# Output rounds two steps earlier, with the row halves turned over at every gap: a fused convolution and ELU layer on one core

## The chip, the cores and the metric

One core of one Trainium2 chip runs the kernel. The metric is the device time of one execution in microseconds (us); for a kernel it is the median over its runs. A core has five engines that work side by side and meet only at semaphores: PE (matrix products; its weight loads, PEld, overlap the products), ACT, DVE, POOL, and SP, which here only issues DMAs. DMAs run on 16 shared DMA engines. PE writes its results to PSUM, from where ACT and DVE read them.

## What is computed

Input `x` is 8 x 4096 tokens of 192 channels. A causal convolution of 7 taps runs along the tokens, with one softmaxed set of taps for each of 8 heads of 24 channels. Its result (32768 tokens x 192) goes through a layer of width 2048 with ELU and back to 192:

```python
w = softmax(weight, axis=-1)                     # 8 heads x 7 taps
out = np.einsum('hk,bskhg->bshg', w, x_unf)      # x_unf: 7 shifted views of x, zero-padded in front
h = x @ w_in                                     # x: the line above, 32768 x 192; w_in: 192 x 2048
g = np.where(h > 0.0, h, np.exp(np.minimum(h, 0.0)) - 1.0)
return g @ w_out                                 # w_out: 2048 x 192
```

## The kernel before

**Tiling.** The tokens are cut into 32 super-tiles `s` (later also `t`) of 1024 tokens, each of two groups `g` of 512. The width 2048 is cut into 16 chunks `q` of 128. A *step* `n` = 16 s + q makes the first product for one super-tile and one chunk, so there are 512 steps. PE's 128 rows are used as two halves of 64 rows that work at the same time (`tile_position`).

**One step.** PE makes a *pair* (L647): six matrix products of 512 columns, three for each token group, out of `att` and `w_in` into one of three slots of `H` in PSUM. ACT takes exp of both groups (L438, two instructions into `E`), POOL clamps them (L355), DVE forms the ELU in `gT` from `E` and from the same slot of `H` (L501). A slot may be written again when DVE has read it (`wait_slot`, semaphore `s_tt`).

**Output rounds.** The second product sums over the 16 chunks. Its unit is the *round* (L677): for a super-tile `t`, a half of its tokens (`half`, 256 tokens of each group), a chunk `q` and a block `kb` of 128 tokens, two matrix products of 192 columns side by side. Row half `rt` multiplies its 64 rows of the chunk's `gT` with its 64 rows of `w_out` and adds into PSUM bank `g` of `ops`. In the first *orientation* row half 0 works for group 0 and row half 1 for group 1; in the second they are exchanged, so that each group gets all 128 rows of the chunk. A bank may not be written by both row halves at once, so a change of orientation (a *turn*) waits until the last round before it has been written (`s_swap`). One half of a super-tile needs 16 chunks x 2 blocks x 2 orientations = 64 rounds, and ACT then copies `ops` to `osb` (L409) and SP issues two output DMAs (L267). `ops` is single: the next half's first round waits for that copy (`s_oev`).

**Order.** The list `order`, written out before the program, sets the order of work on all engines; each engine follows it in turn. Rounds of super-tile `t` go into the gaps between pairs from step 16 (t + 1) + LAG on, with LAG = -1: `HALF_STEPS` gives (10, 10, 6, 6, 10, 11, 11) rounds to seven gaps, the eighth has none, and then the second half follows the same way. All 32 rounds of the first orientation come first (10 + 10 + 6 + 6), so the turn falls between the fourth and the fifth gap, behind a pair.

**Convolution.** A conv (L620) is 40 small matrix products for one group of one super-tile, out of `xg` (tokens, loaded by POOL's DMAs, L307) and `Tr` (taps). ACT copies the result to `csb` (L418), SP writes it to `conv_slots` in DRAM (L711) and, once that has landed, reads it back rearranged into `att` by three DMAs (L279). `m` = 2 s + g - 2 counts the convs; super-tile 0 is made in another way at the start. `CONV_AT` places two convs in each super-tile, at its steps 4 and 12; each splits the eleven-round gap that it falls in (5 rounds, conv, 6 rounds). `EARLY_CONV` places the first three: after the pairs of steps 5, 9 and 16. The first `FREE_CONV` = 2 of them use the two banks of `ops`, which no round needs yet, and ACT copies each in two halves, the second behind the next step's exp; later convs take a slot of `H`. `X_AT` places POOL's loads of `xg`.

**Start.** In the first steps, where there are no rounds, PE gets pairs of idle products (`warm_pair`, L538) that only keep it busy. They write into `ops` and so wait for the copy of an early conv.

**SP's queue** at the start is, in order: the taps, a copy of a part of `w_in` (L704), the write of conv 0 (L711), the three reads of it (L279), the write of conv 1, the three reads of that. Each waits in turn; the pair of step 16 needs all six reads.

**End.** The last half (t = 31, half 1) accumulates in a slot of `H`; ACT copies group 0 (L401), DVE group 1 (L512), and SP and ACT issue one output DMA each.

Of the kernel before, what the change touches and what calls it, by code (L numbers as in the profile page):

```python
# [12 lines left out]
P = 128  # L13
# [13 lines left out]
NXB = 2  # L27
NE = 4
NG3 = 2
LAG = -1  # L30
WCOLS = ((0, 256), (256, 640), (640, 1280), (1280, 2048))
Q_PART = (0,) * 2 + (1,) * 3 + (2,) * 5 + (3,) * 6
WARM = (9, 1)
HALF_STEPS = (10, 10, 6, 6, 10, 11, 11)

CONV_AT = ((4, 1, 1), (12, 2, 0))
EARLY_CONV = {5: (1, 0), 9: (1, 1), 16: (2, 0)}
FREE_CONV = 2
QUAD = 4
XTW = 136  # L40
HALO = 2
XW = 5
X_AT = ((5, 1), (10, 0), (13, 2))

PIECES = (
    ((0, 0, CW, 0), (1, 0, CW, CW), (2, 0, CW, 2 * CW), (3, 0, CW, 3 * CW), (4, 0, 24, 4 * CW)),
# [5 lines left out]
def bass_lightweight_conv__then__act_elu_kernel(  # L52
# [13 lines left out]
    NT = Bsz * S  # L66
    assert S % SUP == 0 and tuple(out.shape) == (NT, D)
    NQ = FF // FC
    NR = 4 * NQ
    assert NQ == 16  # L70
    NS = NT // SUP
    SPB = S // SUP
# [3 lines left out]
    x_flat = x.rearrange("b s d -> (b s) d")  # L76


    steps = []
    slot_of_pair, slot_of_conv, prior = {}, {}, []  # L80
    occupant = [None, None, None]

# [4 lines left out]
        return k  # L87

    order = []
    last_half = (NS - 1, 1)  # L90
    last_slot = None

    def conv_at(s, g):
        m = 2 * s + g - 2
# [1 line left out]
            slot_of_conv[m] = take_slot(("c", m))  # L96
        order.append(("c", m))

    rounds_at = {}
    for t in range(NS):  # L100
        base = NQ * (t + 1) + LAG
        for half in range(2):
            r = 0
            for i, cnt in enumerate(HALF_STEPS):
                rounds_at[base + 8 * half + i] = (t, half, r, r + cnt)
                r += cnt
            assert r == NR
    for n in range(NP + NQ + LAG):
        s, i = divmod(n, NQ)
        if n < NP:  # L110
            slot_of_pair[n] = take_slot(("h", n))
            order.append(("h", n))
        convs = [EARLY_CONV[n]] if n in EARLY_CONV else []
        if s:
            convs += [(s + ahead, g) for at, ahead, g in CONV_AT if at == i and n < NP]
        convs = [(k, g) for k, g in convs if k < NS]
        if n in rounds_at:
            t, half, r0, r1 = rounds_at[n]
            if (t, half) == last_half and r0 == 0:
                last_slot = take_slot(None)  # L120
            mid = (r0 + r1) // 2 if convs else r1
            order.append(("o", t, half, r0, mid))
            for k, g in convs:
                conv_at(k, g)
            if mid < r1:
                order.append(("o", t, half, mid, r1))
        else:
            for k, g in convs:
                conv_at(k, g)


    taps = nc.dram_tensor("conv_taps", (HEADS, ZW), BF16).ap()
    bounce = nc.dram_tensor("conv_slots", (2, 2, P, SUP), BF16).ap()

    with ExitStack() as stack:
# [68 lines left out]
        s_dw = [sema(f"s_dw{i}") for i in range(4)]  # L204
        s_band = sema("s_band")
        s_att = [sema(f"s_att{i}") for i in range(2)]
        s_mm2 = sema("s_mm2")
        s_swap = sema("s_swap")
        s_oev = sema("s_oev")
        s_out = [sema(f"s_out{i}") for i in range(2)]  # L210
# [43 lines left out]
        def conv_read(W, m):  # L254
            W(s_ce, m + 1)

        def out_group(eng, t, half, g):
            b = (2 * t + half) % 2
            row = SUP * t + GS * g + 2 * P * half
            dst = out[row : row + 2 * P, :].rearrange("(k p) d -> p k d", p=P)  # L260
            if t == 0:
                dst = bass.AP(
                    tensor=out.tensor,
                    offset=(GS * half + 1 - g) * D,
                    ap=[[QUAD * D, P], [2 * D, 2], [1, D]],
                )
            eng.dma_start(dst, osb[:, b, g, :, :]).then_inc(s_out[b], 16)  # L267
# [97 lines left out]
        def _scalar(a):  # L365
# [26 lines left out]
            a.activation(  # L392
                att[:, 0, 2, 0 : GS // 2], H[:, 0, 0 : GS // 2], ACT.Copy
            ).then_inc(s_ha)
            def evac(t, half):
                n_half = 2 * t + half
                W(s_mm2, n_half + 1)
                b = n_half % 2
                W(s_out[b], 32 * (n_half // 2))
                if (t, half) == last_half:  # L400
                    a.activation(  # L401
                        osb[:, b, 0, :, :].rearrange("p k d -> p (k d)"),
                        H[:, last_slot % 3, 0 : 2 * D],
                        ACT.Copy,
                    ).then_inc(s_oev)
                    W(s_od, 1)
                    out_group(a, t, half, 1)
                    return
                a.activation(  # L409
                    osb[:, b, :, :, :].rearrange("p g k d -> p g (k d)"),  # L410
                    ops[:, :, 0 : 2 * D],
                    ACT.Copy,
                ).then_inc(s_oev)
# [8 lines left out]
            for item in order:  # L422
                if item[0] == "c":
                    m = item[1]
                    W(s_cv, m + 1)
                    W(s_dw[m % 4], 16 * (m // 4))
                    if m < FREE_CONV:
                        conv_evac(m, 0, 1)
                        late.append(m)
                    else:  # L430
                        conv_evac(m, 0, 2).then_inc(s_ce)
                elif item[0] == "h":
                    n = item[1]
                    k = slot_of_pair[n] % 3
                    W(s_h, n + 1)
                    W(s_tt, 2 * (n - NE) + 2)
                    for u in range(2):
                        a.activation(  # L438
                            E[:, n % NE, u, :], H[:, k, GS * u : GS * (u + 1)], ACT.Exp
                        ).then_inc(s_exp)  # L440
                    if late:
                        conv_evac(late.pop(), 1, 2).then_inc(s_ce)
                else:
                    _, t, half, r0, r1 = item
                    if r1 == NR:
                        evac(t, half)

        @block.vector
        def _vector(v):
# [45 lines left out]
            for n in range(NP):  # L495
                s, q = divmod(n, NQ)
                if s >= NG3:
                    W(s_mm2, 2 * (s - NG3 + 1))
                for u in range(2):
                    W(s_clp, 2 * n + u + 1)  # L500
                    v.scalar_tensor_tensor(  # L501
# [5 lines left out]
                        op1=ALU.max,  # L507
                    ).then_inc(s_tt)
            b = (2 * NS - 1) % 2
            W(s_mm2, 2 * NS)  # L510
            W(s_out[b], 32 * (NS - 1))
            v.tensor_copy(  # L512
                osb[:, b, 1, :, :].rearrange("p k d -> p (k d)"),
                H[:, last_slot % 3, GS : GS + 2 * D],
            ).then_inc(s_od)

        @block.tensor
        def _tensor(pe):
# [61 lines left out]
            for j in range(3):  # L580
# [18 lines left out]
                            tile_position=(HP * r, 0),  # L599
                        )  # L600
                ins.then_inc(s_hc)
            for item in order:
                if item[0] == "c":
                    m = item[1]
                    s, g = divmod(m + 2, 2)
# [23 lines left out]
                elif item[0] == "h":  # L629
                    n = item[1]  # L630
                    s, q = divmod(n, NQ)
                    if n == 0:
                        W(s_ha, 2)
                        W(s_hd, 2)
                    elif n < NQ - 1 and not any(n - 2 <= e < n for e in EARLY_CONV):
                        conv_read(W, sum(e < n for e in EARLY_CONV) - 1)
                        warm_pair(WARM[1])
                    if Q_PART[q] < 3:
# [15 lines left out]
                            )  # L654
                    ins.then_inc(s_h)
                else:
                    _, t, half, r0, r1 = item
                    W(s_w[4], 16)
                    if (t, half) == last_half:
                        acc = H[:, last_slot % 3, :].rearrange("p (g t) -> p g t", g=2)  # L660
                        if r0 == 0:
                            wait_slot(last_slot)
                    else:
                        acc = ops
                        if r0 == 0:
                            conv_read(W, FREE_CONV - 1)
                            W(s_oev, 2 * t + half)
                    for r in range(r0, r1):

                        second, (q, kb) = r // (NR // 2), divmod(r % (NR // 2), 2)  # L670
                        W(s_tt, 2 * (NQ * t + q) + 2)
                        if second:
                            W(s_swap, 2 * (2 * t + half + 1))
                        t0 = 2 * P * half + P * kb
                        for rt in range(2):
                            g = rt ^ second
                            ins = pe.matmul(  # L677
                                acc[:, g, D * kb : D * (kb + 1)],
                                gT[HP * rt : HP * (rt + 1), t % NG3, q, g, t0 : t0 + P],
                                w_out[HP * rt : HP * (rt + 1), q, :],  # L680
                                start=(r == 0),
                                stop=(r == NR - 1),
                                tile_position=(HP * rt, 0),
                            )
                            if r == NR // 2 - 1:
                                ins.then_inc(s_swap)
                    if r1 == NR:
                        ins.then_inc(s_mm2)

        @block.sync  # L690
        def _sync(sy):
# [14 lines left out]
            for item in order:  # L706
# [14 lines left out]
                        W(s_h, NQ * s)  # L721
                        read_att(sy, W, s + 1, 0)
                elif item[0] == "o":
                    _, t, half, r0, r1 = item
                    if r1 < NR:
                        continue
                    W(s_oev, 2 * t + half + 1)
                    for g in range(1 if (t, half) == last_half else 2):
                        out_group(sy, t, half, g)
            for b in range(2):  # L730
                sy.wait_ge(s_out[b], 32 * NS)


# [26 lines left out]
```

## Time and profile before

| | before |
|---|---|
| median of 7 runs | 753.16 us (751.25 to 754.46) |
| the profiled execution: its own time, its span | 753.79 us, 752.0 us |
| busy PE / ACT / DVE / POOL over the span | 737.0 / 646.9 / 635.3 / 662.0 us |
| rounds into `ops`, L677 | 8064 products, 415.3 us |
| pairs, L647 | 3072 products, 407.4 us |
| convs into `H`, L620 | 2400 products, 39.7 us |
| ELU on DVE, L501 | 1024 x 680 ns |
| exp on ACT, L438 | 1024 x 605 ns |

The span runs from the first to the last instruction; the execution's own time has 1.8 us more around it. The end of a product is modelled and products overlap in the pipeline, so what a stretch of PE work costs is read from the start of one group to the start of the next, not from its busy time. PEld is the weight load, which PE pulls ahead of the products where nothing holds it.

### The profile page before, as it was taken

What the parts mean: (1) busy time and instruction counts of PE and PEld (TensorE: products, weight loads), DVE (VectorE), ACT (ScalarE), POOL (GpSimd) and SP (SyncE); (2) the same over time, 40 slices, a digit from 0 to 9 for tenths busy, and PEclk for the clock granted to TensorE, in tenths of its full rate; (3) what the DMA queues carried; (4) which work ended last, traced back from release to release, by engine and by line L of the source; (5) the groups of instructions that cost most, each with busy time, mean ns of one, the idle gap of its engine ahead of it and who ended that gap; (6) DMA issues with size and microseconds to landing.
All of it is one profiled execution on the core that took longest, in us unless ns stands there. A gap on an engine that the chain in (4) does not pass through costs nothing.

```text
span 752.0 us, 32224 instructions
## 1 busy us (share of the span) xinstructions
PE 737.0 (98%) x13858; PEld 512.0 (68%) x13858; DVE 635.3 (84%) x1041; ACT 646.9 (86%) x1163; POOL 662.0 (88%) x1107
## 2 busy tenths in 40 slices
PE   8699999999999999999999999999999999999997
PEld 4376766766766766766667667667667767767676
DVE  5778898898898888898888898888898888888893
ACT  6788888888888888888888888888888888889882
POOL 8779899899899899899898998998998998998882
PEclk9999999999999999999999999999999999999999
DMA  9535345445345345345344345354355344355112
GB/s 176 105 85 117 80 96 118 81 96 116 76 100 117 79 100 108 83 101 117 77 102 103 87 102 114 79 104 95 92 105 111 76 108 91 91 110 107 59 44 65
DMA packets 107006, 72.79 MB, mean 97 GB/s; under 512 B 44520, under 2 KB 106608, under 8 KB 106864
## 3 DMA queue, kind: packets, MB, share of 16 engines
q1 hardware_dynamic: 66224, 54.37, 23.8%
q0 software_dynamic: 40224, 15.78, 19.5%
q8 instruction: 108, 1.77, 1.0%
q10 hardware_dynamic: 416, 0.59, 0.2%
q14 instruction: 34, 0.28, 0.1%
HBM read 44.78 MB, written 41.42 MB: 115 GB/s over the span
## 4 chain that ended last, share of the span: by engine, by line
PE 95%; DMA 2%; DVE 1%; ACT 1%; SPq 0%; issue 0%; POOL 0%
PE ops L677 45%; PE H L647 44%; PE H L620 5%; DVE gT L501 1%; DMA conv_slots<-csb 1%; PE H L677 1%; DMA att<-conv_slots 0%; DMA xf<-in_x_dram 0%; SPq L279 0%; ACT E L438 0%; PE H L589 0%; POOL E L355 0%; PE ops L589 0%; DVE xh L476 0%; ACT csb L418 0%
## 5 line engine op out<-in xcount | busy, mean ns | idle before, releaser
L501 DVE SCALAR_TENSOR_TENSOR gT<-E,H 128x512 f16<-128x512 f32 x1024 | 629.9, 680 | 99.0 <-POOL E L355 91.1
L355 POOL TENSOR_SCALAR E<-E 128x512 f32<-128x512 f32 x1024 | 605.5, 615 | 74.8 <-ACT E L438 72.5
L438 ACT ACTIVATE E<-H 128x512 f32<-128x512 f32 x1024 | 545.9, 605 | 86.0 <-PE H L647 72.5
L677 PEld LDWEIGHTS ops<-w_out,gT 64*128 64x128 f16 x8064 | 342.7, 94 | 109.9 <-ACT osb L409 10.8
L677 PE MATMUL ops<-w_out,gT 64*128 64x192 f16 x8064 | 415.3, 243 | 0.9 <-DVE gT L501 0.9
L647 PE MATMUL H<-att,w_in 64*128 64x512 bf16 x3072 | 407.4, 378 | 6.6 <-DMA att<-conv_slots 2.8
L647 PEld LDWEIGHTS H<-att,w_in 64*128 64x128 bf16 x3072 | 130.2, 94 | 107.0 <-DVE gT L501 4.9
L418 ACT ACTIVATE csb<-H 128x1024 bf16<-128x1024 f32 x60 | 61.4, 1024 | 0.7 <-PE H L620 0.7
L409 ACT ACTIVATE osb<-ops 128x768 f32<-128x768 f32 x63 | 51.5, 817 | 5.1 <-PE ops L677 5.1
L307 POOL DMA_DIRECT2D xg<-in_x_dram x62 | 52.2, 842 | 0.4 <-issue 0.4
L620 PE MATMUL H<-Tr,xg 128*24 128x122 bf16 (+1 forms) x2400 | 39.7, 210 | 0.0
L620 PEld LDWEIGHTS H<-Tr,xg 128*24 128x24 bf16 x2400 | 30.4, 92 | 9.6 <-issue 9.6
L512 DVE COPY osb<-H 128x384 f32<-128x384 f32 x1 | 0.6, 559 | 8.9 <-PE H L677 8.9
L677 PE MATMUL H<-w_out,gT 64*128 64x192 f16 x128 | 5.6, 243 | 0.1
L538 PE MATMUL ops<-zw 64*128 64x512 bf16 x20 | 3.9, 378 | 1.9 <-ACT csb L418 1.9
L677 PEld LDWEIGHTS H<-w_out,gT 64*128 64x128 f16 x128 | 5.2, 94 | 0.3 <-PE H L677 0.3
L533 PE MATMUL ops<-zw 128*128 128x512 bf16 x9 | 4.0, 625 | 1.2 <-DVE zw L451 1.2
L312 POOL DMA_DIRECT2D w_in<-in_moe_w_in_dram x7 | 4.6, 658 | 0.3 <-DMA wh<-in_weight_dram 0.3
L401 ACT ACTIVATE osb<-H 128x384 f32<-128x384 f32 x1 | 0.5, 491 | 4.7 <-PE H L677 4.7
L538 PEld LDWEIGHTS ops<-zw 64*128 64x128 bf16 x20 | 1.0, 94 | 3.7 <-ACT csb L418 2.8
L533 PEld LDWEIGHTS ops<-zw 128*128 128x128 bf16 x9 | 1.2, 142 | 3.2 <-issue 1.9
L418 ACT ACTIVATE csb<-ops 128x512 bf16<-128x512 f32 x4 | 2.5, 619 | 0.0
(46 smaller groups left out, 25.6 us busy)
## 6 DMA issues: line engine op xcount, KB each, us to landing
out_dram<-osb SPq DMA_DIRECT2D x127, 192.0 KB, 2.7
conv_slots<-csb SPq DMA_DIRECT2D x62, 256.0 KB, 2.5
att<-conv_slots SPq DMA_DIRECT2D x186, 64.0 KB
xg<-in_x_dram POOLq DMA_DIRECT2D x31, 240.0 KB, 5.1
xg<-in_x_dram POOLq DMA_DIRECT2D x31, 192.0 KB, 4.5
w_out<-in_moe_w_out_dram POOLq DMA_DIRECT2D x1, 768.0 KB, 14.5
w_in<-in_moe_w_in_dram POOLq DMA_DIRECT2D x2, 240.0 KB, 8.0
xf<-in_x_dram ACTq DMA_DIRECT2D x1, 384.0 KB, 3.1
```

Source lines behind the costliest of these rows:

```text
L307: g.dma_start(xg[:, b, w0:w1, :], src).then_inc(s_x[b][part - 1], 16)
L312: g.dma_start(w_in[HP * r : HP * (r + 1), :, c0:c1], moe_w_in.rearrange("(p j) f -> p j f", j=3)[:, :, c0:c1],).then_inc(s_w[k], 16)
L355: g.tensor_scalar(out=E[:, n % NE, u, :], in0=E[:, n % NE, u, :], scalar1=1.0, scalar2=0.0, op0=ALU.min, op1=ALU.max,).then_inc(s_clp)
L409: a.activation(osb[:, b, :, :, :].rearrange("p g k d -> p g (k d)"), ops[:, :, 0 : 2 * D], ACT.Copy,).then_inc(s_oev)
L418: return a.activation(csb[:, m % 4, b0:b1, :], conv_bank(m)[:, b0:b1, :], ACT.Copy)
L438: a.activation(E[:, n % NE, u, :], H[:, k, GS * u : GS * (u + 1)], ACT.Exp).then_inc(s_exp)
L501: v.scalar_tensor_tensor(out=gT[:, s % NG3, q, u, :], in0=E[:, n % NE, u, :], scalar=1.0, in1=H[:, slot_of_pair[n] % 3, GS * u : GS * (u + ...
L533: pe.matmul(ops[:, 0, :], zw[:, 0:P], zw[:], start=True, stop=True)
L538: pe.matmul(ops[:, r, :], zw[HP * r : HP * (r + 1), 0:P], zw[HP * r : HP * (r + 1), :], start=True, stop=True, tile_position=(HP * r, 0),)
L620: ins = pe.matmul(to[SLOT * q : SLOT * q + CPH, hb, o : o + nc_], xg[:, s % NXB, w, CPH * h : CPH * (h + 1)], Tr[:, h, CW - c0 - nc_ : CW ...
L647: ins = pe.matmul(H[:, k % 3, GS * r : GS * (r + 1)], w_in[HP * r : HP * (r + 1), j, FC * q : FC * (q + 1)], att[HP * r : HP * (r + 1), s ...
L677: ins = pe.matmul(acc[:, g, D * kb : D * (kb + 1)], gT[HP * rt : HP * (rt + 1), t % NG3, q, g, t0 : t0 + P], w_out[HP * rt : HP * (rt + 1) ...
```

## The change

`LAG` becomes -3: rounds of super-tile `t` begin at step 16 t + 13, when only the first chunks of `t` are made. So a half can no longer do its first orientation over all chunks and then the second. `GAPS` replaces `HALF_STEPS`: the orientation turns at each gap, and each orientation goes through the chunks by itself. The sizes are the same (10, 10, 6, 6, 10, 11, 11), but the first of the elevens is written as 5 of one orientation and 6 of the other, with the conv, where there is one, between them. Each uninterrupted group of rounds of one accumulator in one orientation is a *run*; its last two products each raise `s_swap`, and the first round of a run waits for the run before it if that had the other orientation. `s_mm2` goes: who waited for a finished half waits for its last run on `s_swap`.

The convs, their loads and the early convs move with the rounds: `CONV_AT` to steps 2 and 10, `X_AT` from 5, 10, 13 to 3, 8, 11, `EARLY_CONV` to 4, 7 and 10. `FREE_CONV` is 3, so the third conv too uses `ops`. The idle products stop at step 13; six pairs of them remain of ten.

After the last pair all remaining rounds stand in one list, `tail`. The last half (t = 31, half 1) is cut by `kb` into two accumulators in two slots of `H`; the pieces of half 0, block 0 and block 1 alternate, so that half 0 and block 0 are finished 20 and 16 rounds before the end. ACT copies block 0 of both groups in one instruction; of block 1, ACT copies group 0 and DVE group 1. Output DMAs of the last half carry one block each.

```diff
-LAG = -1
+LAG = -3
+GAPS = ((10,), (10,), (6,), (6,), (10,), (5, 6), (11,))
-HALF_STEPS = (10, 10, 6, 6, 10, 11, 11)
-CONV_AT = ((4, 1, 1), (12, 2, 0))
-EARLY_CONV = {5: (1, 0), 9: (1, 1), 16: (2, 0)}
-FREE_CONV = 2
+CONV_AT = ((2, 1, 1), (10, 2, 0))
+EARLY_CONV = {4: (1, 0), 7: (1, 1), 10: (2, 0)}
+FREE_CONV = 3
-X_AT = ((5, 1), (10, 0), (13, 2))
+X_AT = ((3, 1), (8, 0), (11, 2))
...
+    tail = (
+        piece(0, 0, 0, 14, (0, 1)) + piece(1, 0, 0, 12, (0,))
+        + piece(0, 1, 0, 14, (0, 1)) + piece(1, 1, 0, 12, (0,))
+        + piece(1, 0, 0, NQ, (1,))
+        + piece(0, 1, 14, NQ, (0, 1)) + piece(1, 1, 12, NQ, (0,))
+        + piece(0, 0, 14, NQ, (0, 1)) + piece(1, 0, 12, NQ, (0,))
+        + piece(1, 1, 0, NQ, (1,))
+    )
...
+        gaps = list(rounds_at.get(n, ()))
+        if len(gaps) == 2:
+            order.append(("o", gaps.pop(0)))
+        if n in EARLY_CONV:
+            conv_at(*EARLY_CONV[n])
         if s:
...
+            for at, ahead, g in CONV_AT:
+                if at == i and s + ahead < NS:
+                    conv_at(s + ahead, g)
+        if gaps:
+            order.append(("o", gaps[0]))
+    last_slot = [take_slot(None) for _ in range(2)]
+    order.append(("o", tail))
...
-                    elif n < NQ - 1 and not any(n - 2 <= e < n for e in EARLY_CONV):
+                    elif n < NQ + LAG and not any(n - 2 <= e < n for e in EARLY_CONV):
...
-                        if second:
-                            W(s_swap, 2 * (2 * t + half + 1))
+                        if (x_, y) in run_from:
+                            k, prev = run_from[x_, y]
+                            begins = prev is None
+                            if prev is not None:
+                                if runs[prev][0][1] != turned:
+                                    W(s_swap, 2 * (prev + 1))
+                            elif (t, half) == (last, 1):
+                                wait_slot(last_slot[kb])
+                            else:
+                                conv_read(W, FREE_CONV - 1)
+                                W(s_oev, place[key])
...
-                            if r == NR // 2 - 1:
+                            if (x_, y) in run_to:
                                 ins.then_inc(s_swap)
-                    if r1 == NR:
-                        ins.then_inc(s_mm2)
```

In `piece(half, turned, q0, q1, kbs)` the arguments are the half, the orientation, the range of chunks and the blocks; rounds that a gap already made are left out.

## The prediction

> **What bounds the kernel now.** I read the page's first part, then the windows by stage, then the chain of waits at the start, then the order of time in a steady stretch and at the end.
>
> ```profile
> PE 737.0 (98%) x13858; PEld 512.0 (68%) x13858; DVE 635.3 (84%) x1041; ACT 646.9 (86%) x1163; POOL 662.0 (88%) x1107
> ...
> 0.00:35.00 35.00, 24.64 (x310) 11.87 (x310) 24.51 (x48) 23.57 (x47) 28.84 (x50) 1.00 0.88 150
> 35.00:38.26 3.26, 3.26 (x67) 2.45 (x69) 1.07 (x2) 1.74 (x3) 1.19 (x2) 0.62 0.02 5
> 57.58:713.52 655.94, 655.94 (x12494) 458.26 (x12490) 570.38 (x928) 582.58 (x1044) 593.74 (x992) 1.00 0.45 97
> 736.08:748.46 12.38, 11.30 (x258) 10.29 (x254) 3.10 (x7) 2.57 (x6) 2.35 (x4) 1.00 0.21 66
> ```
>
> The windows (columns: window, length, busy PE, PEld, DVE, ACT, POOL, granted clock, DMA share, GB/s) show three stages. From 57 to 713 us PE is never idle, the others have a tenth to spare: only PE work counts. Until 35.0 PE is idle for 10.4 us; work put there costs nothing until the idle time is full. In the tail PE idles 1.1 us. So moving rounds forward does not shorten the middle; it pays only by what falls into the start, and by what the tail loses.
>
> What ends the start is a chain that hardly touches PE:
>
> ```profile
> 20.69 4.88 DMA conv_slots<-csb
> 25.57 0.02 issue
> 25.58 0.67 SPq L279
> ...
> 27.56 2.54 DMA conv_slots<-csb
> ...
> 31.37 3.59 DMA att<-conv_slots
> 34.96 0.05 issue
> 35.00 0.82 PE H L647 x6
> ```
>
> Conv 0 is written to DRAM at 20.69, lands at 25.57, is read; only then does SP write conv 1 (27.56), wait (30.10), read it, and at 34.96 step 16 may start. PE had made its last round by 32.24 and idles 2.77 us. The granted clock then falls to half from 35.75 to 39.17 (0.62 in the window above).
>
> **The change, part by part.** Prices come from this stretch of the steady stage (start, length, work):
>
> ```profile
> 402.06 0.82 PE L647 MATMUL H<-att,w_in 64*128 64x512 bf16 x6
> 402.72 0.66 PE L677 MATMUL ops<-w_out,gT 64*128 64x192 f16 x12
> 403.26 0.82 PE L647 MATMUL H<-att,w_in 64*128 64x512 bf16 x6
> 403.92 0.99 PE L677 MATMUL ops<-w_out,gT 64*128 64x192 f16 x20
> 404.74 0.81 PE L647 MATMUL H<-att,w_in 64*128 64x512 bf16 x6
> 405.39 0.58 PE L677 MATMUL ops<-w_out,gT 64*128 64x192 f16 x10
> 405.89 0.66 PE L620 MATMUL H<-Tr,xg 128*24 128x24 bf16 x40
> 406.49 0.67 PE L677 MATMUL ops<-w_out,gT 64*128 64x192 f16 x12
> 406.99 0.81 PE L647 MATMUL H<-att,w_in 64*128 64x512 bf16 x6
> ```
>
> From start to start, ten rounds take 404.74 - 403.92 = 0.82 us, so a round costs 0.083; a pair 0.65; a conv 0.60, and the eleven rounds around it 0.50 + 0.50 instead of 0.91, so 0.69 in all.
>
> *Work moved ahead of step 16.* Before it stood 10 rounds and two early convs; now 10 + 10 + 6 = 26 rounds and three convs. Out of the PE-bound stage go 16 x 0.083 = 1.33 us and one conv, 0.69: 2.02 us. It is free if step 16 starts no later than now. I went through the start step by step with its rows (pair 0.65, exp 2 x 0.55, clamp and ELU 1.22 per step, csb half 0.6): pair 7 now waits for conv 0's copy until 19.7, conv 1 is over at 21.4, pair 10 waits as before for the copied part of `w_in` (24.3), conv 2 ends at 26.0, step 13's rounds start at 28.75 behind conv 2's second copy (28.7), step 14's at 30.25, step 15's six at 31.75; PE is done at about 32.3, against 32.24 before. Four idle pairs (0.22 each) are gone. So 2.7 us of cover remain; without it each microsecond of lateness costs one.
>
> *Does the chain itself get shorter?* Conv 0's copy ends at about 19.7 instead of 20.66. But SP's write is held elsewhere: in the microsecond from 21 to 22, DMA packets were
>
> ```profile
> q0 software_dynamic: 497, 0.19, 156.1%
> q1 hardware_dynamic: 6, 0.01, 2.6%
> ```
>
> although SP had issued its copy of `w_in` on q1 at 18.07. POOL's loads on q0 land last at 24.88, conv 0 at 25.57. An issue 0.9 us sooner then queues longer and lands at the same time; and conv 1, ready at 24.2 instead of 26.8, stands in SP's queue behind the three reads of conv 0, which wait for that landing. So step 16 stays at 35.0. Bounds: 0 to 0.94 us of gain (the full advance); I take 0, because q0's last landing is the nearer row. The Trainium skill ("DMA: Bandwidth & Descriptors", Queues, rings and completion order) says that an engine takes turns between the queue rows it has work for, packet by packet; an earlier write would then land earlier and the gain would be 0.94 more. The 497 to 6 packets above disagree.
>
> *Clock dip.* The wait is then 35.0 - 32.3 = 2.7 us, as before, and the dip stays: 0. Between 35.66 and 39.36 work that costs 2.25 at full clock took 3.70, so the bound below is -1.45, if the wait shrinks enough.
>
> *Turns.* Each half has now eight runs, so seven waits on `s_swap` at a first round and sixteen increments, against one and three. A turn with nothing between costs what the tail shows: first rounds at 739.72 and 740.06, 0.334 apart instead of 0.082, so 0.25 us. Behind a waiting round stand the rest of its gap and the next pair, and behind that pair ACT. Six of the seven lie behind a pair, as the one at 403.92 does already (preceded by the increments on the last round before 403.26): its ten rounds take 0.82 and the six with increments 0.54, like the six without (401.53 to 402.06, 0.53). Price 0. The Trainium skill ("TensorE: Matmul & The Clock Gate", The cost: per-tile semaphore tail) gives 26.3 ns for each increment on a product; 13 more in 64 halves would make 22 us if each lay on the path. These rows have two on one round and show 0.01 us. The seventh lies behind a conv, 0.08 + 0.60 after the last round's start, more than 0.33: price 0, bounds 0 and 0.25 each. But in super-tiles 30 and 31 no conv is left at three places (step 10; 2 and 10), and there 5 and 6 stand bare: 3 x 0.25 = 0.75 us lost.
>
> *The rest of the middle.* Rounds, pairs, convs, ACT's copies, SP's writes, reads and output DMAs, POOL's `xg` loads (0.84 us of POOL each; seven steps ahead of their conv as before) and the clearing of `xg` all move by the same two steps relative to the rounds, so every queue keeps its order. Two things don't move: SP's read at step 1 now stands one step, not three, ahead of the conv's write; it takes 1.82 us of SP, and there are 14 steps until its data is used, which hide it. And DVE's wait for a finished half before reusing `gT` gets five steps of slack for three. The short waits already there (0.053 in the second gap, 0.04 in the third and fourth, for slots of `H`) stay. Price 0.
>
> *Tail.*
>
> ```profile
> 739.62 0.11 PEld L677 LDWEIGHTS ops<-w_out,gT 64*128 64x128 f16 x4 [1.08 <-DVE gT L501]
> 740.05 2.59 PEld L677 LDWEIGHTS ops<-w_out,gT 64*128 64x128 f16 x64 [0.32 <-PE ops L677]
> 745.60 2.59 PEld L677 LDWEIGHTS H<-w_out,gT 64*128 64x128 f16 x64 [0.32 <-PE H L677]
> ```
>
> Before, the last 128 rounds lose 1.02 us to DVE's last chunk (1.10 between rounds instead of 0.08) and 2 x 0.25 to turns. Now chunks 14 and 15 come 74 rounds (6.1 us) after the last pair, and DVE needed 3.5; other accumulators stand between a run and its turn, at least four rounds (5 x 0.083 = 0.41 > 0.334). Gain 1.5.
>
> *End.* From PE's last product (748.42) to the end are 3.58 us: copy 0.56, DMA 2.5, 0.45. Now ACT's and DVE's last copies are 192 columns (about 0.35 by rows of 512, 384 and 256: 0.2 less) and DMAs of 96 KB, but SP issues four DMAs (0.4 each) of the other pieces before its last, until 0.9 us after PE. Gain 0.1, between -0.4 and +0.5.
>
> Sum: -2.02 + 0.75 - 1.5 - 0.1 = -2.9 us. Against the profiled execution, 753.79 - 2.9 = 750.9; that one lies 0.63 over the median of the runs, so 750.2.
>
> **Rivals.**
>
> 1. *The chain or the dip gives way* (quicker): conv 0 lands with its earlier issue, step 16 starts up to 0.94 sooner, and the wait of 1.8 no longer drops the clock. For it: copy ready earlier, conv 1 ready 2.6 us earlier. Against: q0. 750.2 - 0.94 - 1.45 = 747.8; one of the two alone 748.8 to 749.3.
> 2. *The start is too full* (no change): pairs or copies slip by more than 2.7 us, for ACT has one more split copy there and each of PE's waits for it holds the pair behind. Step 16 at 36.5 to 37 gives back 1.5 to 2: 751.7 to 752.2.
> 3. *Turns behind convs are not covered* (slower). At 406.48 the weight load is not pulled ahead of the first round behind the conv, as it is by 0.2 us behind a pair, so a late `s_swap` would be paid in full. Price up to 0.25 at each of 61 places, 15 us: 765. It decides from 2.9 / 61 = 0.05 us each. Against: 0.68 between, 0.33 needed.
>
> **How the numbers follow.** Forecast 0.56, first rival 0.22, second 0.12, third 0.08, others 0.02. The forecast's own range is 749.2 to 751.4. About 0.2% (1.5 us: below 751.65, above 754.67) can be told from no change. Faster: 0.56 + 0.22 + a third of the second, 0.82. Same: the rest of the second and small cases of the third, 0.10. Slower 0.08. The range runs from both halves of the first rival, 747.6, to the second's end, 752.0.
>
> **What would show it.** Step 16 near 35.0 with 26 rounds and a third conv before it; conv 0's write issued near 19.7 and landing near 25.5; a steady half of 11.32 us as before (397.65 to 409 and on); no wait for `gT` after the last pair, and PE done 8.9 us after that pair's rounds begin. It is wrong if a steady half grows (third rival), or if step 16 moves by over a microsecond.

## The result, and the profile after

The changed kernel takes 750.29 us in the median of 15 runs (749.18 to 753.33), the kernel before 753.2 us (39 runs, 751.17 to 755.6): a ratio of 0.9971, interval 0.9961 to 0.9981, so 2.9 us or 0.3% less. The prediction was 750.2. The number is right; the sum behind it is not quite, as the experiments show. Run again beside another group of runs (e8 below), the same kernel took 752.35 us, 0.9990 (0.9977 to 1.0004) of the kernel before there, so the medians alone don't repeat the gain. The profiled execution after took 750.23 us, its span is 748.5 us.

Windows of the kernel after (columns: window, length, busy PE, PEld, DVE, ACT, POOL with counts, granted clock, DMA share, GB/s):

```profile
0.00:34.70 34.70, 27.38 (x374) 14.12 (x375) 24.06 (x48) 24.56 (x49) 29.17 (x50) 1.00 0.90 159
34.70:38.14 3.44, 3.44 (x55) 2.37 (x56) 1.73 (x4) 2.17 (x4) 1.90 (x4) 1.00 0.08 26
41.13:712.03 670.90, 670.81 (x12743) 473.67 (x12740) 584.40 (x946) 595.07 (x1066) 604.63 (x1012) 1.00 0.44 97
735.87:745.01 9.14, 9.07 (x218) 8.84 (x214) 2.87 (x6) 2.28 (x5) 2.04 (x4) 1.00 0.01 2
```

PE does 2.7 us more ahead of step 16 (27.38 for 24.64), and step 16 starts at 34.70 for 35.00. Behind it the clock is 1.00 where it had been 0.62. The middle is full. From the gap behind the last pair (735.87) to the last product are 9.07 us with no idle time, for 108 rounds. The chain of waits at the start, kernel after (start, length, what):

```profile
20.76 5.38 DMA conv_slots<-csb
26.15 0.02 issue
26.16 0.67 SPq L334
...
28.14 2.67 DMA conv_slots<-csb
...
32.08 2.58 DMA att<-conv_slots
34.66 0.05 issue
34.70 0.82 PE H L706 x6
```

It has the same links as before. Conv 0 was issued at 20.76 and landed only at 26.15, and conv 1's write stood behind the three reads. One of the three bare turns, and the end, in the order of time of the kernel after:

```profile
728.83 1.34 PE L741 MATMUL ops<-w_out,gT 64*128 64x192 f16 x22
...
729.49 0.44 PEld L741 LDWEIGHTS ops<-w_out,gT 64*128 64x128 f16 x12 [0.32 <-PE ops L741]
...
730.00 0.81 PE L706 MATMUL H<-att,w_in 64*128 64x512 bf16 x6
...
745.01 0.36 DVE L572 COPY osb<-H 128x192 f32<-128x192 f32 x1 [6.27 <-PE H L741]
745.01 0.33 ACT L464 ACTIVATE osb<-H 128x192 f32<-128x192 f32 x1 [0.46 <-PE H L741]
```

Eleven rounds take 730.00 - 728.83 = 1.17 us instead of 0.91; the weight load waits 0.32 us for PE's own last products.

A surprise lies in the middle. Before, a half with a conv takes 11.327 us if it is the first of its super-tile and 11.314 if it is the second; after it is 11.314 for the second halves of a super-tile, but 11.366 for the first halves. That is 0.039 us in each of 29 profiled first halves, 1.13 us in all. Kernel after, order of time on PE around a super-tile's first pair:

```profile
418.98 0.82 PE L706 MATMUL H<-att,w_in 64*128 64x512 bf16 x6
419.64 0.66 PE L741 MATMUL ops<-w_out,gT 64*128 64x192 f16 x12
420.26 0.82 PE L706 MATMUL H<-att,w_in 64*128 64x512 bf16 x6
420.91 0.67 PE L741 MATMUL ops<-w_out,gT 64*128 64x192 f16 x12
421.40 0.83 PE L706 MATMUL H<-att,w_in 64*128 64x512 bf16 x6
```

The first six-round gap takes 420.26 - 419.64 = 0.62 us, where the stretch of before had 0.53. The pair at 420.26 is that of step 0; its trace has a separate semaphore instruction of 51 ns on PE's sequencer at 420.155, and the weight load, which waits for `att`, at 420.231.

### The profile page after: what moved, and what is told of

Its sections match the earlier page's. It is cut to its first block, busy times and chain, and to the rows that moved or that the text cites. A ratio compares the mean times of both kernels' runs of the same rounds, so it can differ in the third digit from the quotient of the medians.

```text
span 748.5 us, 32212 instructions
## 1 busy us (share of the span) xinstructions
PE 737.4 (99%) x13850; PEld 517.7 (69%) x13850; DVE 637.7 (85%) x1041; ACT 647.1 (86%) x1165; POOL 661.2 (88%) x1107
## 4 chain that ended last, share of the span: by engine, by line
PE 96%; DMA 2%; ACT 0%; DVE 0%; SPq 0%; issue 0%; POOL 0%
PE ops L741 45%; PE H L706 45%; PE H L679 5%; DMA conv_slots<-csb 1%; PE H L741 1%; DMA xf<-in_x_dram 0%; SPq L334 0%; DMA att<-conv_slots 0%; DVE gT L561 0%; ACT E L499 0%; PE H L648 0%; PE ops L648 0%; PE H L628 0%; ACT csb L479 0%; PE H L616 0%
## 5 line engine op out<-in xcount | busy, mean ns | idle before, releaser
L741 PEld LDWEIGHTS ops<-w_out,gT 64*128 64x128 f16 x8064 | 345.2, 94 | 106.7 <-ACT osb L470 10.8
L741 PE MATMUL ops<-w_out,gT 64*128 64x192 f16 x8064 | 416.8, 243 | 0.3
L706 PE MATMUL H<-att,w_in 64*128 64x512 bf16 x3072 | 407.9, 377 | 4.1 <-DMA att<-conv_slots 1.7
L706 PEld LDWEIGHTS H<-att,w_in 64*128 64x128 bf16 x3072 | 133.8, 94 | 101.5 <-issue 5.0
L741 PE MATMUL H<-w_out,gT 64*128 64x192 f16 x128 | 5.9, 243 | 0.0
L741 PEld LDWEIGHTS H<-w_out,gT 64*128 64x128 f16 x128 | 5.3, 94 | 0.0
L597 PE MATMUL ops<-zw 64*128 64x512 bf16 x12 | 2.3, 380 | 1.6 <-ACT csb L479 1.6
```

The source lines that it names most:

```text
L597: pe.matmul(ops[:, r, :], zw[HP * r : HP * (r + 1), 0:P], zw[HP * r : HP * (r + 1), :], start=True, stop=True, tile_position=(HP * r, 0),)
L706: ins = pe.matmul(H[:, k % 3, GS * r : GS * (r + 1)], w_in[HP * r : HP * (r + 1), j, FC * q : FC * (q + 1)], att[HP * r : HP * (r + 1), s ...
L741: ins = pe.matmul(acc[:, g, d0 : d0 + D], gT[HP * rt : HP * (rt + 1), t % NG3, q, g, t0 : t0 + P], w_out[HP * rt : HP * (rt + 1), q, :], s ...
```

## Experiments

The kernels ran in three groups, each beside runs of the kernel before: e1 to e4 (before: 752.14 us), e5 to e8 (752.88), e9 and e10 (752.80). L706 is the pair, L741 the round in the changed kernel; an edit can move these lines (L709 and L744 in e1, L718 and L753 in e9, L712 and L747 in e7).

| kernel | median (runs), us | ratio to before | step 16 | step 16 to PE's last product |
|---|---|---|---|---|
| before | 753.2 (39) | 1 | 35.00 | 713.41 (clock falls) |
| after | 750.29 (15) | 0.9971 (0.9961 to 0.9981) | 34.70 | 710.24 |
| e1: `att` wait at step 14 | 749.56 (10) | 0.9972 (0.9957 to 0.9987) | 34.82 | 709.18 |
| e2: after, write first | 748.59 (6) | 0.9946 (0.9931 to 0.9960) | 33.96 | 710.29 |
| e3: before, write first | 750.99 (12) | 0.9976 (0.9966 to 0.9986) | 33.32 | 712.15 |
| e4: one load later | 751.01 (12) | 0.9982 (0.9970 to 0.9994) | 35.59 | 710.34 |
| e8: after again | 752.35 (12) | 0.9990 (0.9977 to 1.0004) | 35.37 | 710.26 |
| e5: before, busy wait | 752.48 (11) | 0.9996 (0.9987 to 1.0004) | 35.12 | 712.10 |
| e6: after, busy wait | 750.66 (7) | 0.9970 (0.9958 to 0.9981) | 35.31 | 710.32 |
| e7: three edits together | 747.42 (5) | 0.9924 (0.9910 to 0.9937) | 31.85 | 708.74 |
| e9: third conv late, busy wait | 751.71 (12) | 0.9988 (0.9979 to 0.9998) | 34.49 | 711.26 |
| e10: as e6 | 750.59 (12) | 0.9977 (0.9967 to 0.9987) | 35.66 | 712.00 (clock falls) |

The last two columns are from each kernel's one profile. The last one is the best measure here: without a fall of the clock it repeats within 0.1 us for the same order of work on PE behind step 16 (712.10 and 712.15; 710.24 to 710.34), while medians of the same kernel against before differ by 2 us between groups.

**Why are first halves longer?** e1 takes the wait for `att` off step 0's pair:

```diff
-                    W(s_att[s % 2], 16 * NDMA_ATT * ((s + 1) // 2))
+                    if s < 2:
+                        W(s_att[s % 2], 16 * NDMA_ATT * ((s + 1) // 2))
+                    if s and q == NQ - 2 and s + 1 < NS:
+                        W(s_att[(s + 1) % 2], 16 * NDMA_ATT * ((s + 2) // 2))
```

> The changed kernel, but PE's wait for the six reads of the next super-tile stands at the pair of step 14 instead of step 0 (super-tile 1 keeps it at step 0). Theory (second wait): in the changed kernel step 0's pair stands behind a six-round gap, where its wait for a slot of H is the last to end; because the pair also waits for att, the slot wait is an instruction of its own, and every first half lasts 11.366 us where every second one lasts 11.314. Then first halves fall to 11.326 as before the change, 29 x 0.04 = 1.1 us less: median about 749.2, gap of six rounds before step 0 at 0.537 us instead of 0.627. Rival (the turns, or DVE being slowed by its own new wait at a super-tile's start, make first halves longer): they stay at 11.366 and the median at 750.3.

The same place in e1's order of time:

```profile
419.17 0.66 PE L744 MATMUL ops<-w_out,gT 64*128 64x192 f16 x12
419.71 0.82 PE L709 MATMUL H<-att,w_in 64*128 64x512 bf16 x6
420.36 0.66 PE L744 MATMUL ops<-w_out,gT 64*128 64x192 f16 x12
420.90 0.82 PE L709 MATMUL H<-att,w_in 64*128 64x512 bf16 x6
```

Both six-round gaps take 0.54 us, first halves 11.324 to 11.335, and from step 16 to the end PE needs 709.18 instead of 710.24 us. The second wait is the cause. The median can't show one microsecond between groups of runs (0.9972 against 0.9971 and 0.9990); the profile does.

**What holds step 16?** e2 and e3 exchange two entries of SP's queue, in the kernel after and in the kernel before:

```diff
-                    if m == 0 or g == 1:
-
+                    if m == 1:
+                        read_att(sy, W, s, 0)
+                    if g == 1:
                         read_att(sy, W, s, g)
```

> The changed kernel, but SP writes conv 1 to DRAM before it reads conv 0 back. Theory (SP's order holds the chain): conv 1's copy is ready at about 24.95, its write is issued then instead of 28.1 and lands by 27.5; conv 0's reads go out at 26.2 as now, conv 1's at about 28.1, and step 16 starts at 32.4 to 32.6, where PE is done with its rounds, instead of 34.7. That is 2.1 us: median about 748.2. The wait is then too short to lower the clock in any execution, so no run lies over 750. Rival (the landing of conv 0 and the DMA traffic set the time, not the order): step 16 stays within 0.5 us of 34.7 and the median at 750.

> The kernel before, with the same exchange in SP's queue. There conv 1's copy is ready only at 26.8, so SP now holds conv 0's reads until then: reads of conv 0 from 27.2, of conv 1 from about 29.3, step 16 at 33.8 to 34.4 instead of 35.0. Theory: 0.6 to 1.2 us less, median about 752.2; so the early convs' new places are worth little with the old order of SP and 1.5 us with the new one. Rival (order doesn't matter): 753.2. Rival (conv 0's later reads cost as much as conv 1's earlier write brings): step 16 at 35 or later.

e2's chain:

```profile
19.77 7.02 DMA conv_slots<-csb
26.79 0.02 issue
26.81 0.67 SPq L334
...
30.02 3.90 DMA att<-conv_slots
33.91 0.05 issue
33.96 0.82 PE H L706 x6
```

Conv 1 was written at 23.95 and had landed by 27.26; all six reads follow each other, and the 2.67 us for conv 1 after them are gone from the chain. Step 16 comes at 33.96 in this execution, not at 32.5: conv 0 landed at 26.79, and the last read took 3.90 us. In e7 below, with the same order on SP, the last read took 2.47 us and step 16 started at 31.85. The profiled execution is the slowest of e2's six runs; their median, 748.59, lies near the expected 748.2, and none lies over 750. So the order is one cause. In e3 conv 1 is ready only at 27.3; step 16 came at 33.32, earlier than expected, and the median was 1.15 us below that of the kernel before beside it. The rival that conv 0's later reads eat the gain falls. With the old order the early convs' new places don't show: step 16 started at 35.00 before and at 34.70 to 35.59 with the new places (after, e1, e4, e8). With the new order, 33.96 and 31.85 (e2, e7) stand against 33.32 (e3), one profile each, which leaves open what the places are worth there.

Does conv 0's landing hang on POOL's loads? e4 takes one of them out of the way:

```diff
-            load_x(2, 2)
             for n in range(NP):
                 s, i = divmod(n, NQ)
+                if n == X22_AT:
+                    load_x(2, 2)
```

> The changed kernel, but POOL's load of the second part of xg for super-tile 2 (192 KB) is issued at step 9 instead of before step 0. Theory (conv 0's write waits until POOL's loads before it are through): the loads end about 1 us sooner, conv 0 lands at about 25.0 instead of 26.15, and step 16 starts about 1.1 us sooner, 33.6: median about 749.2. Against that, POOL spends 0.8 us on the issue in the middle of the start, which 2 us of idle PE cover. Rival (conv 0's landing depends on its own issue and the traffic of q1 alone): landing at 26, median 750.3.

It brought nothing (`X22_AT` is 9): conv 0 landed at 25.95, step 16 started at 35.59, and the median was 751.01, not 749.2. `w_out`, now the last load on q0 (POOL's queue) in the start, landed at 25.09 for 25.93 of the load taken away, 0.84 us sooner, but conv 0 landed only 0.20 sooner. In this execution POOL's other loads were later too (`w_in`'s last part at 18.92 instead of 18.08). The load taken away was issued at 26.04 and landed at 30.27, and beside it the write of conv 1 took 3.71 us instead of 2.67. So e4 shows no way to shorten the chain and doesn't support the expectation.

The profiles taken together do: conv 0 was issued between 19.53 (e10) and 22.14 (e3), 2.6 us apart, and landed between 25.49 and 26.79, always within -0.2 to 0.9 us of q0's last load and without regard to its own issue. But there is another candidate. SP's copy of a part of `w_in` stands ahead of conv 0 on q1 (SP's queue); it landed between 23.99 (e7) and 25.27 (e4), and conv 0 0.7 to 2.5 us after it. And from 22 us on the two queues moved side by side. Kernel after, the microsecond from 22 to 23:

```profile
q0 software_dynamic: 276, 0.10, 85.0%
q1 hardware_dynamic: 104, 0.16, 50.6%
```

Whether the loads hold conv 0 directly, or through the copy ahead of it, no edit shows.

**How much of the gain is the clock?** Runs of the kernel after lie in two groups: 11 of the first 15 at 750.9 or below, four at 752.4 or above; in e8, the same kernel run again in the second group, five at 750.93 or below and seven at 751.98 or above. e5 (before) and e6 (after) keep PE busy ahead of step 16:

```diff
+                    k = slot_of_pair[n]
+                    if n == NQ:
+                        wait_slot(k)
+                        for _ in range(8):
+                            for r in range(2):
+                                pe.matmul(
+                                    H[:, k % 3, GS * r : GS * (r + 1)],
+                                    zw[HP * r : HP * (r + 1), 0:P],
+                                    zw[HP * r : HP * (r + 1), :],
+                                    start=True,
+                                    stop=True,
+                                    tile_position=(HP * r, 0),
+                                )
                     W(s_att[s % 2], 16 * NDMA_ATT * ((s + 1) // 2))
-                    k = slot_of_pair[n]
                     wait_slot(k)
```

> The changed kernel itself, beside the others on one chip. Its executions should fall into two groups again, about 750.2 us (clock 0.999 or 1.0) and about 752.5 (0.997 or 0.998), with a quarter in the upper one; the kernel before likewise at 751.8 and 753.8, with a third to three fifths in the upper one.

> The kernel before, but PE fills its wait ahead of step 16 with eight pairs of idle products (8 x 0.216 = 1.7 us) into the slot that step 16 will overwrite; nothing else changes. Theory (part of the change's gain is the clock): the upper group of executions of the kernel before is the one in which the clock falls to half after that wait; with PE kept busy it goes, all executions lie at 751 to 752.7 and the median at about 751.7. Rival (the groups come from something else, the DMA traffic at the start for one): both groups stay, median as before.

> The changed kernel with the same eight pairs of idle products ahead of step 16. Theory: no execution in the upper group, median about 750.1. Against the kernel before with a busy wait the change is then worth 1.6 to 1.7 us, which is what the terms of the profile give without the clock: 2.02 moved work + 1.61 tail - 0.79 bare turns - 1.13 second wait = 1.7. Rival (the moved work is worth more, and the second wait isn't the change's): 2.9 us between the two.

> The changed kernel with the busy wait once more, on the same chip as the other: 750.3 to 750.7 us, 710.3 us from step 16 to PE's last product.

e5 spreads over 751.64 to 753.12, e6 over 749.77 to 751.32; the kernels without the busy wait beside them went up to 754.80 and 753.86. But e5's median, 752.48, missed the expected 751.7 and can't be told from the kernel before by its ratio, 0.9996; its spans can, with a median of 750.2 against 751.1 us. e6's median lies 0.6 over the expected 750.1. Between the medians of the two are 1.82 us, between those of their spans 1.3; in their profiles, from step 16 on, 712.10 - 710.32 = 1.78. That is what the change is worth behind step 16 without a fall of the clock. e8 missed its expectation: not a quarter, but seven of twelve runs lay high.

The clock is not the whole of the upper group. Upper runs lie 2.4 us (first comparison) and 2.9 us (e8) over the lower ones in the median, more than the 1.3 to 1.7 us that one fall costs behind step 16. And e10, the same kernel as e6, has three of twelve runs at 751.83 or above, two of them with a mean granted clock of 1.0. What else lifts them stays open. e10's third, its profiled execution (751.2 us of span), had a fall of the clock in spite of the busy wait. Windows of one clock period (3.41 us) at the wait ahead of step 16, in before, after and e10:

```profile
32.34:35.75 3.41, 0.75 (x10) 0.40 (x11) 1.78 (x3) 0.20 (x1) 0.99 (x2) 1.00 0.11 35
```

```profile
30.26:33.67 3.41, 2.73 (x48) 1.75 (x44) 3.35 (x6) 2.97 (x6) 3.37 (x7) 1.00 0.19 53
33.67:37.08 3.41, 2.38 (x39) 1.67 (x40) 1.70 (x4) 1.46 (x3) 1.57 (x4) 1.00 0.28 94
```

```profile
33.15:36.56 3.41, 1.47 (x18) 0.62 (x16) 1.00 (x2) 0.03 (x1) 0.22 (x1) 1.00 0.39 126
```

Where PE was busy for 0.75 or 1.47 us of such a window, the clock fell to half for the next 3.41 us (35.75 to 39.17; 36.56 to 39.98). Where the wait was split between two windows, 2.73 and 2.38 us busy, it didn't. In between, the busy time alone doesn't decide. e1's clock fell at 7.70, in the start, after a window with 2.05 us (first two lines); e2's stayed full after one with 1.97 (third line):

```profile
4.29:7.70 3.41, 2.05 (x40) 1.42 (x38) 1.51 (x3) 1.67 (x4) 3.41 (x6) 1.00 1.12 162
7.70:11.11 3.41, 3.31 (x32) 2.78 (x34) 0.27 (x1) 1.04 (x2) 3.41 (x5) 0.50 1.05 150
```

```profile
32.17:35.58 3.41, 1.97 (x34) 1.15 (x30) 2.55 (x5) 1.74 (x4) 1.80 (x4) 1.00 0.16 49
```

e1's fall cost nothing behind step 16, so a run's mean clock doesn't tell whether a fall was dear: eight of the 75 runs of the kernel before beside the experiments have a mean clock of 0.997 or 0.998 and yet took less than 751.9 us. The windows begin at another time in each execution, so the same wait lowers the clock in some and not in others.

**Was the early third conv free, and what was it worth?** e9 is e6 with the third conv back in its old place:

```diff
-EARLY_CONV = {4: (1, 0), 7: (1, 1), 10: (2, 0)}
-FREE_CONV = 3
+EARLY_CONV = {4: (1, 0), 7: (1, 1), 16: (2, 0)}
+FREE_CONV = 2
```

> The changed kernel with PE kept busy ahead of step 16 (eight pairs of idle products), and with the third early conv back at step 16 and in a slot of H, as before the change. Theory (the early third conv was free): step 16 starts at the same time after SP's last read has landed, and from there to PE's last product it takes 0.69 us longer than the changed kernel with a busy wait, 711.0 instead of 710.3 us; median 0.7 higher, about 751.3. Rival (the conv's early place delays the start or its later place is covered as well): no difference over 0.2.

e9's order of time on PE behind step 16:

```profile
35.23 0.65 PE L679 MATMUL H<-Tr,xg 128*24 128x122 bf16 x40
35.81 0.67 PE L753 MATMUL ops<-w_out,gT 64*128 64x192 f16 x12
36.31 0.81 PE L718 MATMUL H<-att,w_in 64*128 64x512 bf16 x6
36.96 0.99 PE L753 MATMUL ops<-w_out,gT 64*128 64x192 f16 x20
38.01 0.82 PE L718 MATMUL H<-att,w_in 64*128 64x512 bf16 x6
```

711.26 us instead of 710.32: 0.94, and the medians differ by 1.1. The expected 0.69 is there; the rest is a wait. Ten rounds from 36.96 to 38.01 take 1.05 us instead of 0.82, and the weight load of the pair at 38.01 waits for DVE, which frees its slot of `H`: the conv has taken a slot, and at that point no other pair has run ahead. The kernel before has the same wait, 0.22 us, in the two profiles in which its clock doesn't fall there (e3, e5). The expected equal start did not come: in e9's profile the last read landed at 33.70, but the idle products held step 16 until 34.49, so the medians also contain up to 0.8 us of the busy wait itself.

**A better version.** e7 joins the edits of e1 and e2 and takes away the bare turns:

```diff
+BARE_GAPS = ((10,), (10,), (6,), (6,), (16,), (5,), (11,))
+BARE = ((29, 1), (30, 0), (30, 1))
...
-            for i, sizes in enumerate(GAPS):
+            for i, sizes in enumerate(BARE_GAPS if (t, half) in BARE else GAPS):
...
-                    turned ^= 1
+                    if not (i == 5 and len(sizes) == 1):
+                        turned ^= 1
```

> The changed kernel with three edits: the wait for att at step 14, SP's write of conv 1 ahead of the reads of conv 0, and no bare turns (in the three halves without a conv the gaps are 10, 10, 6, 6, 16, 5, 11, the last two in one orientation). Theory: from 750.2 of the changed kernel without a clock dip, 1.13 + 0.75 (step 16 at 34.0, as with the write alone) + 3 x 0.265 = 2.7 less, about 747.5, and no upper group. Rival: the gap of five rounds doesn't cover the slot wait of the next pair, and 0.2 to 0.3 of each bare turn comes back: 748.1.

```profile
30.75 0.65 PE H L712 x6
31.39 0.50 PE ops L747 x12
31.89 0.78 PE H L712 x6
...
713.82 0.67 PE H L712 x6
714.51 0.61 ACT E L502
...
715.84 1.30 DVE gT L564 x2
717.18 0.82 PE H L712 x6
```

747.42 us, 0.9924 (0.9910 to 0.9937) of the kernel before, over runs from 745.89 (the profiled one) to 747.51; no run lay high. In its chain step 16 (31.89 here) follows the six rounds directly: reads and writes are no longer on the chain. From step 16 on it needs 708.74 us, 1.5 less than the kernel after: 1.06 for the second wait, the rest, about 0.45, for the turns. They cost 0.79, but the wait that the rival named is there: at all three places the second of two pairs in a row now waits 0.26 us for its slot of `H` (1.56 us for the two instead of 1.295). In the chain above the pair at 717.18 waits for the slot of the pair at 713.82, which DVE has still to read. Part of this comes back, as the short slot waits of the next half are gone (ten rounds 0.825 instead of 0.88 us, six 0.495 instead of 0.54).

## Why the prediction was right

From before to after, in the two profiled executions (spans 752.0 and 748.5, 3.5 us apart), by the prediction's terms:

| term | predicted | measured | from |
|---|---|---|---|
| start of step 16 | 0 | -0.30 | 35.00, 34.70; within its spread (34.70 to 35.37 in after, e1, e8) |
| 16 rounds moved ahead of it | -1.33 | -1.33 | rounds counted, 0.083 each; price not tested alone |
| third conv moved ahead of it | -0.69 | -0.94 | e9 against e6; 0.22 of it a slot wait |
| three bare turns | +0.75 | +0.79 | 3 x (1.172 - 0.907) |
| rest of the middle | 0 | +1.06 | e1; 29 x 0.039 = 1.13 in the halves |
| tail | -1.5 | -1.61 | 12.335 - 9.073 less 20 rounds; not tested alone |
| clock | 0 | -1.3 | 713.41 - 712.12 |
| end | -0.1 | -0.06 | 3.60, 3.54 |
| sum | -2.9 | -3.7 | spans: -3.5 |

The measured terms overshoot the spans by 0.2 us, which stays unplaced.

- *The bound and the cover were right.* PE was full from step 16 on, and idle before it behind a chain of DMAs. The 26 rounds and the third conv fitted in front: step 15's rounds began at 32.33 (predicted 31.75; this execution's first pair came 1.35 us later than in the profile before), and the wait that remained was 1.9 us. The second rival, a start too full, did not occur.
- *The chain:* "lands at the same time" held. Issue 20.76, landing 26.15. The prediction took the row from 21 to 22 for the whole stretch. q1 moved nothing from the copy's issue at 18.09 to 22, but from 22 to 25 it moved 434 packets beside q0's 704. So the turns between queues that the Trainium skill states ("DMA: Bandwidth & Descriptors", Queues, rings and completion order) agree with the trace from 22 us on, where both get packets through; why they don't show before, no run tells.
- *The turns* cost nothing where work lies between: gaps behind a pair take 0.825 us for ten rounds as before, and behind a conv six rounds take 0.506 in both kernels. The third rival falls, and with it the price for each increment that the prediction weighed from the Trainium skill ("TensorE: Matmul & The Clock Gate", The cost: per-tile semaphore tail): 13 more in each half left the second halves at 11.314.
- *The step that failed* is the one of the middle: "The short waits already there (0.053 in the second gap, 0.04 in the third and fourth, for slots of `H`) stay. Price 0." They stay, but the change moves step 0's pair from a ten-round gap, where the slot wait is long over, to a six-round gap, where it is the last to end. This pair also waits for `att`. Its slot wait is then an instruction of its own, and the weight load can only start after it: 0.09 us more, of which about 0.05 comes back right behind it (the next six rounds take 0.494 instead of 0.537). The list of waits on each PE instruction showed both waits at this pair; the prediction moved steps "relative to the rounds" and didn't ask which pairs carry more than one.
- *The clock* was priced at 0 because the wait was to stay as long. In the profile after the wait was 1.9 us and the clock didn't fall, so this half of the first rival came true there. A fall is worth 1.3 us behind step 16 (1.7 in e10), and some executions of both kernels have it. In the first comparison, by the times alone, 4 of 15 runs of the kernel after and 23 of 39 of the kernel before lay in their upper groups (above 752.4 and above 753), which made good the 1.1 us that the middle lost; in e8 seven of twelve lay high, and the ratio was 0.9990. So the agreement of 750.2 with 750.29 is partly luck: behind step 16, and without a fall of the clock, the change is worth about 1.8 us, not 2.9.

## What to carry to other kernels

Work moved into a wait is free only up to the wait's end, and what ends the wait may be found elsewhere: here exchanging two entries of a DMA queue, in the kernel before, was worth about as much as the whole reordering (step 16 at 33.32 and 712.15 us behind it, against 35 and 710.3). When an order is shifted, look for the instructions that carry two waits and ask at which of them the last wait to end has moved. And a median over runs that fall into two groups moves with the share of the groups; a stretch of the profile that the clock and the start don't touch tells a microsecond apart.

## What the runs showed of the hardware

- A product that waits for two semaphores had one of the waits as an instruction of its own on PE (51 ns), which cost 0.09 us from the gap's length (0.627 against 0.537) where it was the last to end, and nothing where it was not.
- The granted clock changed only at the ends of periods of 3.41 us that follow each other without a break (5.03 to 35.75 is nine of them). It fell after periods with PE busy for 0.75, 1.47 and 2.05 us (before, e10, e1) and stayed after 1.97 and 2.34 us (e2, e8), so the busy time alone doesn't set it. The full clock also began at different times: where the trace's first record of it lies at 4.1 to 5.9 us and lasts, the first pair started at 10.74 to 11.10, and where it lies at 9.5 to 10.7, at 12.03 to 12.98. Step 16 doesn't follow this: 35.00 with the full clock at 5.03, 34.70 with 9.78.
- A DMA queue stood still while another was worked off, and then shared with it: in the kernel after SP's copy on q1, issued at 18.09, moved nothing until 22 (506 packets on q0 and none on q1 from 21 to 22), and from 22 to 25 q1 moved 434 packets and q0 704. In all twelve profiles q1 began between 21 and 23 us.
- The last read of 64 KB back from DRAM ahead of step 16 took between 2.37 us (e3) and 3.90 us (e2) from issue to landing. How many reads stand in a row doesn't set it: as the last of six it took 2.37, 2.47 (e7) and 3.90, as the last of three 2.58 (after) and 3.59 (before).
